# A fused Mamba-2 scan and SiLU MLP on one Trainium2 core: weight clipping on GpSimd, a wider-row load of C, and a later product for one unit

## The chip, the core and the metric

The kernel runs on one core of one Trainium2 chip. The core has five engines that run side by side and meet at semaphores: TensorE (PE in the profile, its weight loads PEld), VectorE (DVE), ScalarE (ACT), GpSimd (POOL) and SyncE (SP), which issues most DMAs here. The metric is the device time of one execution in microseconds (us); lower is better. The kernel before has a median of 353.54 us in three runs (353.08 to 353.58).

## The reference

Two blocks follow each other. The first is a state-space scan over 4 batches, 8 heads and 768 tokens with head dimension D = 32 and state dimension N = 16; the second is a two-matrix MLP with SiLU between.

```python
# x (4, 8, 768, 32), a (4, 8, 768), B and C (4, 8, 768, 16): float32
log_a = log(clip(a, 1e-6, 1)); state = 0
for each chunk of tokens:
    cum   = cumsum(log_a in the chunk)
    L     = exp(cum_i - cum_j) for i >= j, else 0
    y     = ((C B^T) * L) x  +  (C state) * exp(cum_i)      # "decay" of C by the prefix product
    state = exp(sum log_a) * state + sum_j B_j x_j exp(cum_last - cum_j)
# bridge: (batch, head, token, D) -> (batch*token, head*D), 3072 x 256
h = y @ w_in            # w_in  (256, 2048), float64
g = h / (1 + exp(-h))
out = g @ w_out         # w_out (2048, 256), float64; out 3072 x 256 in float32
```

The two weight matrices arrive as float64, so the kernel turns each of them into float32 on the chip, bit by bit.

## The kernel before

The 3072 tokens are cut into 12 units of 256 tokens, three to a batch (`UPB = 3`). Unit 0 opens batch 0, units 1 and 2 continue it, unit 3 opens batch 1. For each unit the scan part makes `XM[u]` (the y of that unit), and two MLP products follow. The first MLP product is `f_s1`; the second comes in steps of one matmul from a generator and is taken with `f_s2(n)`. Weights are handled in 16 pieces, 0 to 7 of `w_in` and 8 to 15 of `w_out`. `f_s1(g, j)` needs `w_in` piece j.

Loads. `load_n` brings B (i = 0) or C (i = 1) with tokens on partitions, so each run in memory is one head's 16 numbers of one token: 64 bytes. `load_t` brings them with 8 tokens to a partition row: 512 bytes to a run.

```python
def load_n(u, i, q):
    b, t0 = at(u)
    if i == 0:
        t = bn[u] = loads.tile([128, 2, H, N], FP32, name="bn")
    else:
        t = tbc[u] = loads.tile([128, 2, 2, 8, N], FP32, name="tbc")[:, 0]
    for k in range(2):
        q.dma_start(out=t[:, k], in_=(B, C)[i][b, :, t0 + 128 * k:t0 + 128 * k + 128].rearrange("h p n -> p h n"))

def load_t(u, i, q):
    b, t0 = at(u)
    if i == 0:
        tbc[u] = loads.tile([128, 2, 2, 8, N], FP32, name="tbc")
    for g in range(4):
        q.dma_start(out=tbc[u][32 * g:32 * g + 32, i],
                    in_=(B, C)[i][b, 2 * g:2 * g + 2, t0:t0 + UT].rearrange("e (t r) n -> t e r n", r=8))

def load_unit(u):
    load_pa(u, nc.sync)
    if 0 < u < UPB:
        load_n(u, 1, nc.sync)
    else:
        load_t(u, 0, nc.sync)
        load_t(u, 1, nc.sync)
    load_ab(u, nc.sync)
    load_n(u, 0, nc.sync)
    load_x(u, nc.sync)
```

Weights. Two ScalarE operations make a magnitude `u` and a low part `v`; VectorE clips u, shifts it and merges the sign into v; GpSimd adds the two as integers.

```python
def w_size(n):
    u = wu[n] = wtp.tile([128, 2, WF], FP32, name="wu")
    v = wv[n] = wtp.tile([128, 2, WF], FP32, name="wv")
    nc.scalar.activation(u, raw[n][:, :, :, 1].bitcast(FP32), AF.Abs)
    nc.scalar.activation(v, raw[n][:, :, :, 0], AF.Copy, scale=2.0 ** -51, bias=2.0)

def w_bits(n, parts=1):
    # ... u, v, hi and dst are the tiles of piece n
    nc.vector.tensor_scalar(out=u, in0=u, scalar1=LEAST, scalar2=MOST, op0=ALU.max, op1=ALU.min)       # clip, L174
    nc.vector.tensor_scalar(out=u, in0=u, scalar1=3, scalar2=None, op0=ALU.logical_shift_left)         # shift, L176
    nc.vector.scalar_tensor_tensor(out=v, in0=hi, scalar=0x80000000, in1=v,
                                   op0=ALU.bitwise_and, op1=ALU.bitwise_or)                            # sign, L178
    for i in range(parts):
        nc.gpsimd.tensor_tensor(out=dst[:, :, fs].bitcast(U32), in0=u[:, :, fs], in1=v[:, :, fs], op=ALU.add)  # L182
    if n + RAW < len(W):
        load_w(n + RAW, nc.sync)
```

The scan's use of B and C. `f_T` is a VectorE transpose, `f_TP` a TensorE transpose into PSUM (units 1 and 2 alone), `f_C` multiplies C by the prefix product of a. `f_P0`, `f_P1` make that prefix product, `f_E0`, `f_E1`, `f_Ek` make the decay matrix E by scans on VectorE, `f_B` decays B on GpSimd, `f_D0` and `f_G0` are small matmuls, `f_S` carries the state, `f_SM` masks it on ScalarE, `f_M` multiplies E into the product, `f_Y` is the matmul for y, and `f_X` copies y out of PSUM.

```python
def f_T(u, i):
    t = (BH, CT)[i][u] = sc.tile([128, UT], FP32, name=("bh", "ct")[i])
    nc.vector.transpose(out=t.rearrange("p (t r) -> p r t", r=8), in_=tbc[u][:, i].rearrange("p e r n -> p r e n"))
    if i == 1:
        tbc.pop(u)

def f_TP(u):
    tp = ps_o.tile([128, 512], FP32, name="o_ps")
    for i, t in enumerate((bn[u], tbc.pop(u))):
        for k in range(2):
            nc.tensor.transpose(out=tp[:, 256 * i + 128 * k:256 * i + 128 * k + 128],
                                in_=t[:, k].rearrange("p h n -> p (h n)"), identity=ident)
    BH[u] = sc.tile([128, UT], FP32, name="bh")
    nc.scalar.activation(BH[u], tp[:, 0:256], AF.Copy)
    CT[u] = tp[:, 256:512]

def f_C(u):
    CW[u] = sc.tile([128, UT], FP32, name="cw")
    engine = nc.vector if 0 < u < UPB else nc.gpsimd
    engine.tensor_tensor(out=CW[u].rearrange("p (c t) -> p c t", t=Q),
                         in0=CT.pop(u).rearrange("p (c t) -> p c t", t=Q), in1=PFX[u][:, :, 1:], op=ALU.mult)
```

The order of issue at the start is written by hand, and each engine keeps it:

```python
# ... unit 0's transposes, G0, E, B, D0, P, C before this
f_S(0); f_SM(0)
for k in range(2): f_M(0, k)
w_size(0); w_bits(0, 2)
f_Ab(1, 0); w_size(1); busy(4, 17)
f_Y(0); f_Ab(1, 1); f_X(0)
w_size(2); w_bits(1); load_unit(2)
f_s1(0, 0)
f_Ek(1, 0); f_TP(1)
for e in range(2): f_T2(1, e)
f_s1(0, 1)
f_Ek(1, 1); f_B(1); w_bits(2); f_C(1); f_D0(1, True); f_G0(1); f_S(1); f_SM(1)
w_size(3)
for k in range(2): f_M(1, k)
f_s1(0, 2); w_size(4); w_bits(3); w_bits(4)
f_Y(1); f_X(1); w_size(5)
f_s1(0, 3)
# then f_s1 of units 0 and 1 in turn, with weight pieces (s = w_size, b = w_bits) and unit 2's scan between:
steps = ((1, 0, "b5 s6"), (1, 1, "b6 s7"), (1, 2, "b7 s8"), (1, 3, "b8"), (0, 4, "E D"),
         (1, 4, ""), (0, 5, "T C s9"), (1, 5, "b9 s10"), (0, 6, "G"), (1, 6, "b10 s11"),
         (0, 7, "Y b11 s12"), (1, 7, "b12 s13"))
```

The stage in which units 4 and 5 are scanned while unit 3 goes through its first product:

```python
for j in range(8):
    # ...
    f_s1(3, j)
    scan_piece(4, j, ("TE", "DCS", "G", "YS", "", "", "", ""))
    scan_piece(5, j, ("", "", "T", "E", "DCS", "G", "YS", ""))
    # ...
    f_s2(2 if j in (5, 6) else 4)
```

Of the kernel before, what the change touches and what calls it, by code (L numbers as in the profile page):

```python
# [8 lines left out]
FP32 = mybir.dt.float32  # L9
U32 = mybir.dt.uint32  # L10
BF16 = mybir.dt.bfloat16
AF = mybir.ActivationFunctionType
ALU = mybir.AluOpType
# [8 lines left out]
def kernel(  # L22
# [26 lines left out]
    Q = 64  # L49
# [46 lines left out]
                        in_=bass.AP(tensor=a.tensor, offset=a.offset + b * H * S + t0 + t * Q,  # L96
                                    ap=[[0, 64], [S, H], [1, Q]]))

    def load_n(u, i, q):

        b, t0 = at(u)
        if i == 0:
            t = bn[u] = loads.tile([128, 2, H, N], FP32, name="bn")
        else:
            t = tbc[u] = loads.tile([128, 2, 2, 8, N], FP32, name="tbc")[:, 0]
        for k in range(2):
            q.dma_start(out=t[:, k], in_=(B, C)[i][b, :, t0 + 128 * k:t0 + 128 * k + 128].rearrange("h p n -> p h n"))  # L107

    def load_t(u, i, q):

        b, t0 = at(u)
        if i == 0:
            tbc[u] = loads.tile([128, 2, 2, 8, N], FP32, name="tbc")
        for g in range(4):
            q.dma_start(out=tbc[u][32 * g:32 * g + 32, i],
                        in_=(B, C)[i][b, 2 * g:2 * g + 2, t0:t0 + UT].rearrange("e (t r) n -> t e r n", r=8))
# [6 lines left out]

    def load_unit(u):
        load_pa(u, nc.sync)
        if 0 < u < UPB:
            load_n(u, 1, nc.sync)
        else:
            load_t(u, 0, nc.sync)
            load_t(u, 1, nc.sync)  # L130
        load_ab(u, nc.sync)
        load_n(u, 0, nc.sync)
        load_x(u, nc.sync)

    w_in_sb = const.tile([128, KC, d_ff], FP32, name="w_in_sb")
# [24 lines left out]
    def w_size(n):  # L160
        if n in raw:
# [3 lines that stand above are left out]

            nc.scalar.activation(v, raw[n][:, :, :, 0], AF.Copy, scale=2.0 ** -51, bias=2.0)

    def w_bits(n, parts=1):
        dst = w_piece(n)[1]
        if n in raw:  # L170
            u, v, hi = wu.pop(n), wv.pop(n).bitcast(U32), raw[n][:, :, :, 1]


            nc.vector.tensor_scalar(out=u, in0=u, scalar1=LEAST, scalar2=MOST, op0=ALU.max, op1=ALU.min)  # L174
            u = u.bitcast(U32)
            nc.vector.tensor_scalar(out=u, in0=u, scalar1=3, scalar2=None, op0=ALU.logical_shift_left)  # L176

            nc.vector.scalar_tensor_tensor(out=v, in0=hi, scalar=0x80000000, in1=v,  # L178
                                           op0=ALU.bitwise_and, op1=ALU.bitwise_or)
            for i in range(parts):  # L180
                fs = slice(WF // parts * i, WF // parts * (i + 1))
# [3 lines that stand above are left out]
# [10 lines left out]
    pz01, one01, pfx01 = (flat[:, 8 * UT + QZ * i:8 * UT + QZ * (i + 1)] for i in range(3))  # L195
    load_t(0, 0, nc.scalar)
    load_t(0, 1, nc.sync)
    load_n(0, 0, nc.scalar)
    nc.sync.dma_start(out=pa01, in_=bass.AP(tensor=a.tensor, offset=a.offset, ap=[[S, H], [0, N], [1, 2 * UT]]))
    load_x(0, nc.sync)  # L200
    for n in range(3):
        load_w(n, nc.sync)
    load_n(1, 0, nc.sync)
    load_n(1, 1, nc.sync)
    load_x(1, nc.sync)

    mark = const.tile([1, RAW], U32, name="mark")
# [107 lines left out]
    def f_Ek(u, k):  # L315
        scan_E(u, H * k, H, ab.pop((u, k)))
# [26 lines left out]
# [7 lines that stand above are left out]
    def f_TP(u):  # L350

        tp = ps_o.tile([128, 512], FP32, name="o_ps")
        for i, t in enumerate((bn[u], tbc.pop(u))):
            for k in range(2):
                nc.tensor.transpose(out=tp[:, 256 * i + 128 * k:256 * i + 128 * k + 128],
                                    in_=t[:, k].rearrange("p h n -> p (h n)"), identity=ident)
        BH[u] = sc.tile([128, UT], FP32, name="bh")
        nc.scalar.activation(BH[u], tp[:, 0:256], AF.Copy)
        CT[u] = tp[:, 256:512]

    def f_T2(u, e):

# [4 lines left out]
    def f_C(u):  # L367

        CW[u] = sc.tile([128, UT], FP32, name="cw")
        engine = nc.vector if 0 < u < UPB else nc.gpsimd  # L370
        engine.tensor_tensor(out=CW[u].rearrange("p (c t) -> p c t", t=Q),
                             in0=CT.pop(u).rearrange("p (c t) -> p c t", t=Q), in1=PFX[u][:, :, 1:], op=ALU.mult)

    def f_D0(u, early=False):

# [41 lines left out]
    def f_S(u, t0=0, t1=4):  # L417

        first, last = u % UPB == 0, u % UPB == UPB - 1
        if first and t0 == 0:  # L420
            ST[u] = sc2.tile([128, 4, 64], FP32, name="st")
        if not last and t1 == 4:
            ST[u + 1] = sc2.tile([128, 4, 64], FP32, name="st")
        for t in range(t0, min(t1, 3 if last else 4)):
            k, c = divmod(t, 2)
            o = ST[u][:, t + 1] if t < 3 else ST[u + 1][:, 0]
            if first and t == 0:
                nc.vector.tensor_copy(out=o, in_=BX[u][c][:, k])
            else:
                nc.vector.scalar_tensor_tensor(out=o, in0=ST[u][:, t], scalar=PFX[u][:, t, Q:],  # L430
                                               in1=BX[u][c][:, k], op0=ALU.mult, op1=ALU.add)

    def f_SM(u):

        t0 = 1 if u % UPB == 0 else 0
        SM[u] = sc.tile([128, 4, 64], FP32, name="sm")
        for e in range(2):
            nc.scalar.activation(SM[u][:, t0:, 32 * e:32 * e + 32], ST[u][:, t0:, 32 * e:32 * e + 32],
                                 AF.Copy, scale=par[:, e:e + 1])
# [43 lines left out]
    def f_s1(g, j):  # L483
        if j == 0:
            GTS[g] = new_g()
        xm = XM[g].rearrange("p (w c) t -> p w (c t)", w=2)
        hp = ps_h.tile([128, 2, UT], FP32, name="hp")
        for i in range(2):
            f = 2 * j + i
            for kc in range(KC):  # L490
                nc.tensor.matmul(out=hp[:, i], lhsT=w_in_sb[:, kc, f * 128:(f + 1) * 128],  # L491
                                 rhs=xm[:, kc], start=(kc == 0), stop=(kc == KC - 1))
        nc.scalar.activation(GTS[g][:, :, j], hp, AF.Silu)  # L493
        if j == 7:
            XM.pop(g)
# [243 lines left out]
    def scan_piece(u, j, plan):  # L739
        for what in plan[j]:  # L740
            if what == "E":
                f_P(u)
                f_E(u)
            elif what == "T":
                if u < UPB:
                    f_TP(u)
                else:
                    f_T(u, 0)
                    f_T(u, 1)
                f_T2(u, 0)  # L750
                f_T2(u, 1)
            elif what == "t":
                f_T(u, 0)
                f_T(u, 1)
            elif what == "B":
                f_B(u)
                f_C(u)
            elif what == "D":
                f_B(u)
            elif what == "C":  # L760
                f_C(u)
            elif what == "S":
                f_SW(len(SW))
            elif what == "G":
                f_GMD(u)
            elif what == "Y":
                f_Y(u)
                f_X(u)
# [34 lines left out]
    f_D0(0, True)  # L803
    f_P01()
    f_C(0)
    f_S(0)
    f_SM(0)
    for k in range(2):
        f_M(0, k)
    w_size(0)  # L810
    w_bits(0, 2)
    f_Ab(1, 0)
    w_size(1)
    busy(4, 17)
    f_Y(0)
    f_Ab(1, 1)
    f_X(0)
    w_size(2)
    w_bits(1)
    load_unit(2)  # L820
    f_s1(0, 0)
    f_Ek(1, 0)
    f_TP(1)
    for e in range(2):
        f_T2(1, e)
    f_s1(0, 1)
    f_Ek(1, 1)
    f_B(1)
    w_bits(2)
    f_C(1)  # L830
    f_D0(1, True)
    f_G0(1)
    f_S(1)
# [62 lines left out]
    for j in range(8):  # L896
        waiting, PEND[:] = PEND[:], []
        f_s1(3, j)
        scan_piece(4, j, ("TE", "DCS", "G", "YS", "", "", "", ""))
        scan_piece(5, j, ("", "", "T", "E", "DCS", "G", "YS", ""))  # L900
        scan_piece(6, j, ("",) * 7 + ("t",))
        if j == 7:
            for i in range(4):
                f_XT(2, i)

        f_s2(2 if j in (5, 6) else 4)
        if j == 3:
            f_SO(3)
        outputs(waiting)
        if j == 5:  # L910
            f_T1(1, 0)
            f_T1(1, 1)
            f_TS(1, 3, 0)
        if j in (2, 5):
            load_unit(6 + j // 3)
# [67 lines left out]
```

## Time and profile before

| what | value |
|---|---|
| time, median of three runs | 353.54 us |
| span of the profiled execution | 353.3 us |
| TensorE busy | 343.8 us (97%) |
| VectorE busy | 204.4 us (58%) |
| ScalarE busy | 162.0 us (46%) |
| GpSimd busy | 111.5 us (32%) |
| mean DMA rate | 121 GB/s |
| TensorE busy from 0 to 30 us of the span | 25.8 us |
| TensorE busy from 60 to 340 us | 279.76 us |

How to read it. A busy share is an average over the whole span. The last two rows, from the stage table, cut it in two: the opening has gaps on TensorE, the long middle hardly any. In the timeline each row gives the start in us, the time from the first start to the last end of the merged instructions, the engine, the line of the kernel, what is written from what, and how many; in square brackets stands how long the engine had been idle and who released it. A row marked SPq is the issue of a DMA on SyncE's queue, not the transfer.

### The profile page before, as it was taken

To read this page: it belongs to the slowest core of one execution; us is meant where nothing else is said; L and a number is where in the kernel's file an instruction comes from. 1 tells how busy PE (TensorE), PEld (TensorE's weight loads), DVE (VectorE), ACT (ScalarE), POOL (GpSimd) and SP (SyncE) were. 2 spreads that over 40 slices of the span, in tenths; PEclk is the share of its full clock that TensorE was granted. 3 is DMA by queue.
4 is the path that set the end of the run, shared out by engine and by line. 5 is a ranking of instruction groups with operands and counts; after the bars stand their busy time and mean duration, and the time that the engine had idled before them with its cause. 6 is when DMAs were issued, how large, how long until landed. Compare 5 with 4: busy or idle time off the path is not lost.

```text
span 353.3 us, 8349 instructions
## 1 busy us (share of the span) xinstructions
PE 343.8 (97%) x3308; PEld 287.5 (81%) x3308; DVE 204.4 (58%) x408; ACT 162.0 (46%) x394; POOL 111.5 (32%) x137
## 2 busy tenths in 40 slices
PE   8979999999999999999999999999999999999995
PEld 3658778888888888888888888888888888888883
DVE  6997879978586663553664563564652232234821
ACT  2567487233323645454645445544545454453100
POOL 4344335554085041244041244041234112051200
PEclk9999999999999999999999999999999999999999
DMA  6986895699649398958179956057404237522202
GB/s 107 225 243 161 174 371 108 125 194 210 132 99 154 81 185 164 184 104 147 32 146 185 172 98 105 16 98 143 92 2 74 51 61 142 90 46 38 36 4 46
DMA packets 117376, 42.79 MB, mean 121 GB/s; under 512 B 102488, under 2 KB 109144, under 8 KB 117336
## 3 DMA queue, kind: packets, MB, share of 16 engines
q1 hardware_dynamic: 110328, 25.67, 34.7%
q0 software_dynamic: 4464, 16.25, 24.9%
q10 hardware_dynamic: 2544, 0.33, 0.6%
q8 instruction: 26, 0.43, 0.6%
q14 instruction: 14, 0.11, 0.1%
HBM read 22.83 MB, written 3.15 MB: 74 GB/s over the span
## 4 chain that ended last, share of the span: by engine, by line
PE 75%; DVE 9%; DMA 8%; SPq 5%; issue 2%; ACT 0%; ACTq 0%; DVEq 0%
PE o_ps L627 32%; PE hp L682 28%; PE hp L491 4%; PE hp L627 3%; DMA out_dram<-ot 2%; DMA ab<-in_a_dram 2%; SPq L95 2%; PE o_ps L613 2%; PE gy L467 2%; DVE E L303 1%; DVE E L415 1%; DMA raw<-in_moe_w_out_dram 1%; SPq L107 1%; PE gy L458 1%; DMA gT<-in_a_dram 1%
## 5 line engine op out<-in xcount | busy, mean ns | idle before, releaser
L685 DVE TENSOR_TENSOR gT<-hp,p 128x256 f32<-128x256 f32 x64 | 26.9, 420 | 73.8 <-ACT p L696 37.9
L491 PE MATMUL hp<-XM,w_in_sb 128*128 128x256 f32 x256 | 59.6, 382 | 2.0 <-POOL w_in_sb L182 2.0
L627 PE MATMUL o_ps<-gT,w_out_sb 128*128 128x256 f32 x240 | 60.4, 379 | 0.0
L688 ACT ACTIVATE gT<-gT 128x256 f32<-128x256 f32 x96 | 39.7, 414 | 44.0 <-DVE gT L685 43.9
L491 PEld LDWEIGHTS hp<-XM,w_in_sb 128*128 128x128 f32 x256 | 47.9, 190 | 10.0 <-POOL w_in_sb L182 3.3
L682 PE MATMUL hp<-raw 128*128 128x256 f32 x192 | 52.7, 380 | 0.0
L544 POOL TENSOR_TENSOR ps<-ps 128x256 f32<-128x256 f32 x35 | 29.2, 835 | 72.3 <-ACT ps L574 71.0
L627 PEld LDWEIGHTS o_ps<-gT,w_out_sb 128*128 128x128 f32 x240 | 45.4, 190 | 6.3
L539 POOL DMA_DIRECT2D gT<-gT x31 | 27.4, 921 | 64.9 <-PE hp L682 22.3
L682 PEld LDWEIGHTS hp<-raw 128*128 128x128 f32 x192 | 36.2, 190 | 5.4 <-POOL ps L544 0.6
L696 ACT ACTIVATE p<-hp 128x256 f32<-128x256 f32 x64 | 24.5, 383 | 27.5 <-PE hp L682 26.1
L685 DVE TENSOR_TENSOR gT<-hp,u 128x256 f32<-128x256 f32 x32 | 13.6, 425 | 39.3 <-PE hp L682 39.3
L682 PE MATMUL hp<-XM,w_in_sb 128*128 128x256 f32 x128 | 34.1, 389 | 0.0
L493 ACT ACTIVATE gT<-hp 128x512 f32<-128x512 f32 x32 | 19.0, 594 | 28.3 <-PE hp L491 28.2
L682 PEld LDWEIGHTS hp<-XM,w_in_sb 128*128 128x128 f32 x128 | 23.3, 190 | 4.3 <-issue 1.0
L303 DVE TENSOR_TENSOR_SCAN E<-ab,diag 128x256 f32<-128x256 f32 (+1 forms) x32 | 25.6, 842 | 0.4
L574 ACT ACTIVATE ps<-o_ps 128x256 f32<-128x256 f32 x38 | 14.4, 382 | 23.9 <-PE o_ps L627 22.2
L340 POOL TENSOR_TENSOR BT<-bn,E 128x256 f32<-128x256 f32 x12 | 9.0, 748 | 50.2 <-DVE E L303 48.9
L627 PE MATMUL o_ps<-gT,wu 128*128 128x256 f32 x88 | 22.4, 380 | 0.0
L627 PE MATMUL o_ps<-gT,wv 128*128 128x256 f32 x88 | 22.2, 380 | 0.0
L627 PE MATMUL o_ps<-gT,raw 128*128 128x256 f32 x80 | 20.6, 382 | 0.0
L682 PE MATMUL hp<-raw,w_in_sb 128*128 128x256 f32 x64 | 19.1, 380 | 0.0
(125 smaller groups left out, 518.7 us busy)
## 6 DMA issues: line engine op xcount, KB each, us to landing
gT<-gT POOLq DMA_DIRECT2D x31, 512.0 KB, 6.0
ab<-in_a_dram SPq DMA_DIRECT2D x40, 128.0 KB, 3.9
raw<-in_moe_w_in_dram SPq DMA_DIRECT2D x8, 512.0 KB, 6.3
raw<-in_moe_w_out_dram SPq DMA_DIRECT2D x8, 512.0 KB, 6.5
xt<-in_x_dram SPq DMA_DIRECT2D x24, 128.0 KB, 5.7
out_dram<-ot SPq DMA_DIRECT2D x92, 32.0 KB, 2.5
bn<-in_B_dram SPq DMA_DIRECT2D x22, 64.0 KB, 4.8
tbc<-in_C_dram SPq DMA_DIRECT2D x40, 32.0 KB, 1.8
```

What stands on the lines that cost most here:

```text
L303: nc.vector.tensor_tensor_scan(out=E[u].rearrange("p k h t -> p (k h t)")[:, Q * g0:Q * (g0 + n)], data0=t.rearrange("p g t -> p (g t)"), ...
L340: engine.tensor_tensor(out=BT[u], in0=bn[u], in1=E[u][:, :, :, Q - 1:Q].to_broadcast([128, 2, H, N]), op=ALU.mult)
L491: nc.tensor.matmul(out=hp[:, i], lhsT=w_in_sb[:, kc, f * 128:(f + 1) * 128], rhs=xm[:, kc], start=(kc == 0), stop=(kc == KC - 1))
L493: nc.scalar.activation(GTS[g][:, :, j], hp, AF.Silu)
L539: nc.gpsimd.dma_start(out=o[:, js], in_=a[:, js], accum_op=ALU.add)
L544: engine.tensor_tensor(out=o, in0=p, in1=q, op=op)
L574: nc.scalar.activation(pn, on, AF.Copy)
L627: nc.tensor.matmul(out=o, lhsT=w(j), rhs=g()[:, j], start=(j == 0), stop=(j == last))
L682: nc.tensor.matmul(out=o, lhsT=w, rhs=x_, start=start, stop=True, skip_group_check=True)
L685: nc.vector.tensor_tensor(out=o, in0=p, in1=q, op=ALU.add)
L688: nc.scalar.activation(o, i, AF.Silu)
L696: nc.scalar.activation(o, i, AF.Copy)
```

## The change

It has four parts. First, GpSimd clips the weight pieces 0, 1 and 2 in place of VectorE, and the ScalarE operations of pieces 0 and 1 move ahead in the order of issue. Second, C of units 1 and 2 (unit 3 had it already) is loaded in runs of 512 bytes by `load_t` in place of 64 bytes by `load_n`. Third, that C is then transposed by VectorE into SBUF in place of by TensorE into PSUM, and GpSimd in place of VectorE multiplies it by the prefix product. Fourth, in the stage of units 4 and 5, two matmuls of the second product are issued ahead of the scan's parts in each step, so that the scan's matmuls, unit 5's y among them, come later in TensorE's order. It is meant to take work from VectorE at the start, to shorten the loads of units 1 and 2, and to let unit 5's y find its inputs ready.

The diff, with blank lines taken out:

```diff
--- before.py
+++ after.py
@@ -96,20 +96,17 @@
                         in_=bass.AP(tensor=a.tensor, offset=a.offset + b * H * S + t0 + t * Q,
                                     ap=[[0, 64], [S, H], [1, Q]]))
-    def load_n(u, i, q):
+    def load_n(u, q):
         b, t0 = at(u)
-        if i == 0:
-            t = bn[u] = loads.tile([128, 2, H, N], FP32, name="bn")
-        else:
-            t = tbc[u] = loads.tile([128, 2, 2, 8, N], FP32, name="tbc")[:, 0]
+        bn[u] = loads.tile([128, 2, H, N], FP32, name="bn")
         for k in range(2):
-            q.dma_start(out=t[:, k], in_=(B, C)[i][b, :, t0 + 128 * k:t0 + 128 * k + 128].rearrange("h p n -> p h n"))
+            q.dma_start(out=bn[u][:, k], in_=B[b, :, t0 + 128 * k:t0 + 128 * k + 128].rearrange("h p n -> p h n"))
     def load_t(u, i, q):
         b, t0 = at(u)
-        if i == 0:
+        if u not in tbc:
             tbc[u] = loads.tile([128, 2, 2, 8, N], FP32, name="tbc")
         for g in range(4):
             q.dma_start(out=tbc[u][32 * g:32 * g + 32, i],
@@ -123,13 +120,11 @@
     def load_unit(u):
         load_pa(u, nc.sync)
-        if 0 < u < UPB:
-            load_n(u, 1, nc.sync)
-        else:
+        if u >= UPB:
             load_t(u, 0, nc.sync)
-            load_t(u, 1, nc.sync)
+        load_t(u, 1, nc.sync)
         load_ab(u, nc.sync)
-        load_n(u, 0, nc.sync)
+        load_n(u, nc.sync)
         load_x(u, nc.sync)
     w_in_sb = const.tile([128, KC, d_ff], FP32, name="w_in_sb")
@@ -165,14 +160,18 @@
             nc.scalar.activation(v, raw[n][:, :, :, 0], AF.Copy, scale=2.0 ** -51, bias=2.0)
-    def w_bits(n, parts=1):
+    def w_clip(n, engine):
+
+
+        if n in raw:
+            engine.tensor_scalar(out=wu[n], in0=wu[n], scalar1=LEAST, scalar2=MOST, op0=ALU.max, op1=ALU.min)
+
+    def w_bits(n, parts=1, clip=True):
         dst = w_piece(n)[1]
         if n in raw:
-            u, v, hi = wu.pop(n), wv.pop(n).bitcast(U32), raw[n][:, :, :, 1]
-
-
-            nc.vector.tensor_scalar(out=u, in0=u, scalar1=LEAST, scalar2=MOST, op0=ALU.max, op1=ALU.min)
-            u = u.bitcast(U32)
+            if clip:
+                w_clip(n, nc.vector)
+            u, v, hi = wu.pop(n).bitcast(U32), wv.pop(n).bitcast(U32), raw[n][:, :, :, 1]
             nc.vector.tensor_scalar(out=u, in0=u, scalar1=3, scalar2=None, op0=ALU.logical_shift_left)
             nc.vector.scalar_tensor_tensor(out=v, in0=hi, scalar=0x80000000, in1=v,
@@ -195,13 +194,13 @@
     pz01, one01, pfx01 = (flat[:, 8 * UT + QZ * i:8 * UT + QZ * (i + 1)] for i in range(3))
     load_t(0, 0, nc.scalar)
     load_t(0, 1, nc.sync)
-    load_n(0, 0, nc.scalar)
+    load_n(0, nc.scalar)
     nc.sync.dma_start(out=pa01, in_=bass.AP(tensor=a.tensor, offset=a.offset, ap=[[S, H], [0, N], [1, 2 * UT]]))
     load_x(0, nc.sync)
     for n in range(3):
         load_w(n, nc.sync)
-    load_n(1, 0, nc.sync)
-    load_n(1, 1, nc.sync)
+    load_n(1, nc.sync)
+    load_t(1, 1, nc.sync)
     load_x(1, nc.sync)
     mark = const.tile([1, RAW], U32, name="mark")
@@ -350,13 +349,11 @@
     def f_TP(u):
         tp = ps_o.tile([128, 512], FP32, name="o_ps")
-        for i, t in enumerate((bn[u], tbc.pop(u))):
-            for k in range(2):
-                nc.tensor.transpose(out=tp[:, 256 * i + 128 * k:256 * i + 128 * k + 128],
-                                    in_=t[:, k].rearrange("p h n -> p (h n)"), identity=ident)
+        for k in range(2):
+            nc.tensor.transpose(out=tp[:, 128 * k:128 * k + 128], in_=bn[u][:, k].rearrange("p h n -> p (h n)"),
+                                identity=ident)
         BH[u] = sc.tile([128, UT], FP32, name="bh")
         nc.scalar.activation(BH[u], tp[:, 0:256], AF.Copy)
-        CT[u] = tp[:, 256:512]
     def f_T2(u, e):
@@ -367,9 +364,8 @@
     def f_C(u):
         CW[u] = sc.tile([128, UT], FP32, name="cw")
-        engine = nc.vector if 0 < u < UPB else nc.gpsimd
-        engine.tensor_tensor(out=CW[u].rearrange("p (c t) -> p c t", t=Q),
-                             in0=CT.pop(u).rearrange("p (c t) -> p c t", t=Q), in1=PFX[u][:, :, 1:], op=ALU.mult)
+        nc.gpsimd.tensor_tensor(out=CW[u].rearrange("p (c t) -> p c t", t=Q),
+                                in0=CT.pop(u).rearrange("p (c t) -> p c t", t=Q), in1=PFX[u][:, :, 1:], op=ALU.mult)
     def f_D0(u, early=False):
@@ -746,7 +742,7 @@
                     f_TP(u)
                 else:
                     f_T(u, 0)
-                    f_T(u, 1)
+                f_T(u, 1)
                 f_T2(u, 0)
                 f_T2(u, 1)
             elif what == "t":
@@ -803,31 +799,35 @@
     f_D0(0, True)
     f_P01()
     f_C(0)
+    w_size(0)
+    w_clip(0, nc.gpsimd)
     f_S(0)
     f_SM(0)
+    w_size(1)
+    w_clip(1, nc.gpsimd)
     for k in range(2):
         f_M(0, k)
-    w_size(0)
-    w_bits(0, 2)
+    w_bits(0, 2, False)
     f_Ab(1, 0)
-    w_size(1)
     busy(4, 17)
     f_Y(0)
     f_Ab(1, 1)
     f_X(0)
     w_size(2)
-    w_bits(1)
+    w_bits(1, 1, False)
     load_unit(2)
     f_s1(0, 0)
+    f_T(1, 1)
     f_Ek(1, 0)
     f_TP(1)
     for e in range(2):
         f_T2(1, e)
+    f_C(1)
+    w_clip(2, nc.gpsimd)
     f_s1(0, 1)
     f_Ek(1, 1)
     f_B(1)
-    w_bits(2)
-    f_C(1)
+    w_bits(2, 1, False)
     f_D0(1, True)
     f_G0(1)
     f_S(1)
@@ -896,14 +896,15 @@
     for j in range(8):
         waiting, PEND[:] = PEND[:], []
         f_s1(3, j)
+
+        f_s2(2)
         scan_piece(4, j, ("TE", "DCS", "G", "YS", "", "", "", ""))
         scan_piece(5, j, ("", "", "T", "E", "DCS", "G", "YS", ""))
         scan_piece(6, j, ("",) * 7 + ("t",))
         if j == 7:
             for i in range(4):
                 f_XT(2, i)
-
-        f_s2(2 if j in (5, 6) else 4)
+        f_s2(0 if j in (5, 6) else 2)
         if j == 3:
             f_SO(3)
         outputs(waiting)
```

## The prediction

> **What bounds the kernel now.** I read the page's busy shares first, then the stage table, then TensorE's timeline at each gap, then the waits and the SyncE queue behind them.
>
> ```profile
> PE 343.8 (97%) x3308; PEld 287.5 (81%) x3308; DVE 204.4 (58%) x408; ACT 162.0 (46%) x394; POOL 111.5 (32%) x137
> ...
> 15.00:20.00 5.00, 4.66 (x22) 3.29 (x20) 4.97 (x7) 2.89 (x7) 3.13 (x4) 1.00 0.94 161
> 20.00:25.00 5.00, 4.07 (x142) 3.12 (x144) 4.60 (x12) 3.32 (x7) 1.37 (x2) 1.00 0.71 233
> 25.00:30.00 5.00, 4.27 (x62) 3.67 (x49) 4.54 (x6) 3.09 (x7) 2.54 (x2) 1.00 0.90 271
> 30.00:35.00 5.00, 5.00 (x25) 4.41 (x24) 3.02 (x7) 4.55 (x9) 2.56 (x2) 1.00 0.50 103
> ```
>
> The columns after the stage and its length are PE, PEld, DVE, ACT and POOL. TensorE is the bound: 97% over all and 279.76 of 280 us from 60 to 340. Only gaps can be won, and work that leaves TensorE inside the full stretch. From 15 to 30 us VectorE is at 4.5 to 5.0 of 5 and TensorE is not: VectorE paces the start. TensorE's timeline names the gaps:
>
> ```profile
> 18.14 1.99 PE L491 MATMUL hp<-XM,w_in_sb 128*128 128x256 f32 x8 [0.34 <-POOL w_in_sb L182]
> ...
> 22.07 1.99 PE L491 MATMUL hp<-XM,w_in_sb 128*128 128x256 f32 x8 [0.94 <-POOL w_in_sb L182]
> ...
> 26.21 1.99 PE L491 MATMUL hp<-XM,w_in_sb 128*128 128x256 f32 x8 [0.73 <-POOL w_in_sb L182]
> ...
> 40.59 0.75 PE L355 MATMUL o_ps<-ident,bn 128*128 128x128 f32 x2 [0.30 <-DMA bn<-in_B_dram]
> 41.18 0.38 PE L355 MATMUL o_ps<-ident,tbc 128*128 128x128 f32 x2
> 41.39 3.62 PE L491 MATMUL hp<-XM,w_in_sb 128*128 128x256 f32 x16
> ...
> 50.15 0.69 PE L458 MATMUL gy<-cw,sm 32*64 32x64 f32 x32 [0.50 <-DVE E L415]
> ...
> 107.96 0.69 PE L458 MATMUL gy<-cw,sm 32*64 32x64 f32 x32 [0.24 <-DVE E L415]
> ```
>
> Three waits for weight pieces 1, 2 and 3 make 0.34 + 0.94 + 0.73 = 2.01 us; unit 2 has 0.30 (B not landed) and 0.50 (its E late); unit 5 has 0.24. Together 3.05 us: with the transposes taken out, nearly all that this change can bring. Behind unit 2's gaps stands SyncE's queue:
>
> ```profile
> 10.53 4.62 SPq L107 DMA_DIRECT2D tbc<-in_C_dram  x2
> ...
> 25.50 4.97 SPq L107 DMA_DIRECT2D tbc<-in_C_dram  x2
> 30.52 5.94 SPq L95 DMA_DIRECT2D ab<-in_a_dram  x4
> 36.50 1.25 SPq L107 DMA_DIRECT2D bn<-in_B_dram  x2
> 37.79 2.82 SPq L122 DMA_DIRECT2D xt<-in_x_dram  x2
> 40.71 4.13 SPq L156 DMA_DIRECT2D raw<-in_moe_w_out_dram  x7
> ```
>
> The two issues of C take 4.62 and 4.97 us, and what follows waits in line: unit 2's a and B, and pieces 9 to 15. The chain of waits runs through just these rows.
>
> [...] the two-input add of 128x512 takes 1303 ns, a one-input select of that size 670. The clip itself has not run there yet[...]. [...] the shift (L176) takes 0.43 us alone and 1.39 us beside an add. [...] four 512-byte C issues of later units take 1.83 us, two 64-byte ones 4.6 to 5.0. [...] Here GpSimd's rows show SBUF operands only.
>
> **The change, part by part.**
>
> Clips. Between the end of unit 0's E product (12.98) and the start of unit 1's (22.13) VectorE loses three clips of 0.42 and the decay of C of 0.41, and gains a transpose of 0.64: 1.26 + 0.41 - 0.64 = 1.03 us less. GpSimd gains 3 x 0.75 + 0.68 = 2.9 us; its rows between 11.4 and 22.0 hold 1.72 + 1.27 + 0.68 + 1.26 = 4.9 of 10.6 us, so there is room. But the order costs. Unit 0's x is there at 10.07 (its matmul's wait ends); the weights follow it, and 512 KB at the 380 GB/s that the DMA view shows then is 1.4 us, so piece 0 lands at about 11.45. ScalarE, which did the mask first at 11.50, now does the two operations of piece 0 (12.05 to 13.27 before, so 1.22 us) and then the mask: done at 13.3 in place of 12.14. Unit 0's y started at 13.10, so it loses about 0.25. Piece 1's magnitude follows at 14.0, GpSimd clips it to about 14.8, and only then adds piece 0's first half, to 15.65 (0.86 each; before 15.32). The first product then starts near 15.7, not 15.39: 0.3 later. VectorE's shift of piece 1 waits for the same clip and then falls beside the adds[...]. GpSimd also has C and clip 2 (1.4 us) ahead of unit 1's B, which frees D0 and the state. So of the 1.03 us perhaps a third comes through to the product at 26.21. I take **0.3 us**, between a loss of 0.3 and a gain of 0.9.
>
> C in wide rows. Each C load of units 1 and 2 goes from two issues (4.62, 4.97) to four of about 0.43, 1.7 us: 2.9 and 3.2 us less on the queue, some 6 us in all for what follows unit 2's C, less what the backlog of weight transfers takes back. B of unit 2 is ready before 40: **0.30**. Its a lands before 40.45, where VectorE waited 0.78, and piece 9, for which ScalarE waited 3.02 to 45.79, comes some 5 us earlier; piece 9's bits no longer hold back the state and E of unit 2, and the gap before its y goes: **0.50**.
>
> Transposes. From the start at 40.59 to the next product at 41.39 four transposes took 0.80 us, in the full stretch. Two remain, about 0.35: **0.45**. Unit 1's pair (17.42 to 17.80) lies in the gap before 18.14: nothing. VectorE's extra 0.64 - 0.40 for unit 2 lies beside products.
>
> Unit 5's y. Both the small matmuls that start its state and its y move back by two matmuls (0.87 us). The state step began at 105.71, late because VectorE was at work on another sum until 105.78, not because of TensorE (done at 104.93); so E stays ready at about 107.8 while y comes at 108.6: **0.24** gained.
>
> Sum: 0.3 + 0.30 + 0.50 + 0.45 + 0.24 = 1.79 us. 353.54 - 1.79 = 351.75; I say 351.7. From 60 us on nothing else moves but by being earlier; the last 13 us stay as they are.
>
> **Rivals.** (1) *GpSimd becomes the pace-setter of the start*: the clips sit in its order ahead of adds and of unit 1's B, and ScalarE's new order delays the mask. For it: the waits just worked out, and VectorE, busy 4.5 to 5.0 of every 5 us there[...]. Against it: GpSimd's room. It would take the 0.3 and up to 0.5 more: about 352.5. (2) *VectorE's saving comes through whole*: piece 0 lands by 10.8, clips take 0.67. Then products 1 to 3 gain about 1 us: 351.0, and down to 350.4 if earlier weights help too. (3) *The earlier loads are hidden anyway, or collide*: the queue's stall on C may be the backlog of 2 MB of weights issued from 22.0 to 24.7, and the next issue then stalls in its place. Then unit 2's 0.8 shrinks to about 0.3: 352.3. Against it: 4.62 us on C of unit 1 while fewer weights waited. (4) *TensorE, being earlier, meets work that is not ready* from 50 to 80 us, where VectorE is at 98% in the first ten. Against it: the last weight piece is added at 64.5 and used after 67; the sum for the fifth product ends at 68.1 and is used at 70.66.
>
> **Range and chances.** The parts that don't depend on order (unit 2's transposes, unit 5) give 0.7; all gaps closed give 3.5. A loss at the start of 0.5 with unit 2's gain missed leaves 353.0; everything right gives 350.4. Two per cent would be 7 us, twice all gaps, so both outer chances are near nothing.
>
> **What would show it.** TensorE's waits for weight pieces, 2.01 us before, should stay between 1 and 2.3; the product of 26.21 should start between 25.3 and 26.5. The C issues should be four of 0.4 each; no wait for B at 40; the gap before unit 2's y gone; no 0.24 before unit 5's y; TensorE's transposes reading B alone. GpSimd's clip should take 0.65 to 0.85 us. The prediction is wrong if that clip is two-input slow (1.3 us), if the first product starts after 16.3, if the wide C load takes as long to issue as the narrow one, or if a new wait opens between 50 and 80 us.

## The result: slower by 1.7%, and the profile after

The changed kernel takes 358.74 us (358.35 to 360.07, five runs) where the kernel before takes 353.08 (352.87 to 353.58): a ratio of 1.0167, 95% interval 1.0143 to 1.0192. The prediction was 351.7, between 350.4 and 353.0. It missed in size and in sign.

The page of the changed kernel, its TensorE row and the row of the clock granted to TensorE:

```profile
PE 346.6 (97%) x3303; PEld 289.1 (81%) x3304; DVE 203.8 (57%) x405; ACT 162.4 (45%) x394; POOL 117.0 (33%) x142
...
PEclk9989999999989999999999999999999999999999
```

The busy share is the same 97%. But there are fewer matmuls and more busy time than before, and the clock row has two slices of 8 (the 3rd is the opening, the 12th lies near 100 us). TensorE's timeline has the gaps that answer to those shown before:

```profile
16.25 2.00 PE L487 MATMUL hp<-XM,w_in_sb 128*128 128x256 f32 x8 [1.03 <-POOL w_in_sb L181]
18.09 0.38 PE L353 MATMUL o_ps<-ident,bn 128*128 128x128 f32 x2
19.33 1.97 PE L487 MATMUL hp<-XM,w_in_sb 128*128 128x256 f32 x8 [0.85 <-DVE E L302]
22.16 0.46 PE L385 MATMUL hp<-xt,BT 64*32 64x64 f32 x32 [0.87 <-POOL BT L339]
...
24.39 3.51 PE L487 MATMUL hp<-XM,w_in_sb 128*128 128x256 f32 x8 [1.14 <-POOL w_in_sb L181]
27.82 0.69 PE L454 MATMUL gy<-cw,sm 32*64 32x64 f32 x32
...
29.23 14.08 PE L487 MATMUL hp<-XM,w_in_sb 128*128 128x256 f32 x64
43.15 0.38 PE L353 MATMUL o_ps<-ident,bn 128*128 128x128 f32 x2
43.37 3.62 PE L487 MATMUL hp<-XM,w_in_sb 128*128 128x256 f32 x16
...
99.11 2.06 PE L623 MATMUL o_ps<-gT,w_out_sb 128*128 128x256 f32 x4 [2.14 <-ACT ps L570]
101.11 1.13 PE L454 MATMUL gy<-cw,sm 32*64 32x64 f32 x32
...
113.98 0.69 PE L454 MATMUL gy<-cw,sm 32*64 32x64 f32 x32
```

Piece 3's product starts at 29.23, not 26.21. The product of piece 2 takes 3.51 us where each other one takes 1.97 to 2.00: half of the lateness is speed, not waiting. Unit 2 has no gap (43.15, 43.37) and unit 5's y has none (113.98), as forecast. But there is a wait of 2.14 us at 99.11 that the kernel before did not have, and again the two matmuls after it (four instructions) are slow: 2.06 us, where two others of this kernel take 1.13 (at 94.12).

The same timeline for GpSimd and VectorE in the opening (L167 is the clip, L175 the shift, L181 the add, L339 unit 1's B):

```profile
11.70 3.81 POOL L167 TENSOR_SCALAR wu<-wu 128x512 f32<-128x512 f32 x2 [0.67 <-ACT wu L159]
...
13.65 0.83 DVE L175 TENSOR_SCALAR wu<-wu 128x512 uint32<-128x512 uint32 x1 [1.00 <-POOL wu L167]
...
15.48 1.59 POOL L181 TENSOR_TENSOR w_in_sb<-wu,wv 128x256 uint32<-128x256 uint32 x2
15.54 0.95 DVE L175 TENSOR_SCALAR wu<-wu 128x512 uint32<-128x512 uint32 x1 [0.45 <-POOL wu L167]
...
19.58 1.92 POOL L167 TENSOR_SCALAR wu<-wu 128x512 f32<-128x512 f32 x1
21.46 0.65 POOL L339 TENSOR_TENSOR BT<-bn,E 128x256 f32<-128x256 f32 x1
21.54 0.86 DVE L175 TENSOR_SCALAR wu<-wu 128x512 uint32<-128x512 uint32 x1 [1.24 <-POOL wu L167]
```

One clip takes 1.92 us on GpSimd, against 0.42 on VectorE. Two of them stand back to back ahead of piece 0's adds, and the shift of piece 0 starts only when the first is over (13.65); the third stands ahead of unit 1's B, which its matmuls wait for until 22.16 (20.06 before). VectorE, which was to be relieved, stands idle 1.00, 0.45 and 1.24 us for the clips.

At 97 us it is ScalarE's order that explains the wait. Its timeline in the changed kernel:

```profile
95.30 0.69 ACT L434 ACTIVATE sm<-st,par 128x128 f32<-128x128 f32 x2 [2.35 <-DVE st L426]
97.89 0.91 ACT L362 ACTIVATE ce<-ct,par 128x256 f32<-128x256 f32 x2 [1.89 <-DVE ct L345]
98.70 0.36 ACT L570 ACTIVATE ps<-o_ps 128x256 f32<-128x256 f32 x1
```

The copy that empties `o_ps` (L570) stands behind the two operations on unit 5's transposed C (L362), which wait for VectorE until 97.89. There is only one `o_ps` buffer, and two matmuls of the next segment now come ahead of unit 4's y and need it 1.4 us earlier than before. In the kernel before the same copy stood behind the same two operations, and came just in time for the matmul at 96.78:

```profile
95.50 0.91 ACT L365 ACTIVATE ce<-ct,par 128x256 f32<-128x256 f32 x2 [1.90 <-PE hp L491]
96.31 0.36 ACT L574 ACTIVATE ps<-o_ps 128x256 f32<-128x256 f32 x1
96.78 1.99 PE L627 MATMUL o_ps<-gT,w_out_sb 128*128 128x256 f32 x8
```

Counted from the start of the product ahead of it (93.55 before, 95.08 after), the copy is 0.86 us later (2.76 before, 3.62 after), because unit 4's small matmuls, and with them VectorE's state step and transposes, also stand behind two matmuls more. 1.4 and 0.9, less the 0.1 there was to spare, make 2.2, where 2.14 was measured.

The stage table of this execution for both places (after the stage and its length: PE, PEld, DVE, ACT, POOL, then the granted clock):

```profile
22.00:25.00 3.00, 1.70 (x66) 1.28 (x67) 2.83 (x8) 1.02 (x3) 1.37 (x2) 0.85 0.60 193
25.00:28.00 3.00, 3.00 (x18) 2.18 (x20) 1.76 (x4) 0.87 (x3) 1.13 (x1) 0.59 0.83 251
...
96.00:100.00 4.00, 1.86 (x7) 1.32 (x6) 3.97 (x8) 1.66 (x4) 0.86 (x1) 0.90 0.82 141
100.00:104.00 4.00, 4.00 (x103) 2.97 (x103) 1.69 (x3) 0.60 (x1) 2.80 (x4) 0.68 0.41 101
```

Right after each stretch in which TensorE was about half idle (busy 1.70 of 3 us and 1.86 of 4), the clock is 0.59 and 0.68 for some microseconds. No single gap between matmuls in these stretches is longer than the 2.14 us at 99.11. What brings the lower clock on is not shown by this trace; the fillers below test whether the idle time does.

### The profile page after: what moved, and what is told of

It is laid out like the page before. It is cut to its first block, busy times and chain, and to the rows that moved or that the text cites. A ratio compares the mean times of both kernels' runs of the same rounds, so it can differ in the third digit from the quotient of the medians.

```text
span 358.2 us, 8352 instructions
## 1 busy us (share of the span) xinstructions
PE 346.6 (97%) x3303; PEld 289.1 (81%) x3304; DVE 203.8 (57%) x405; ACT 162.4 (45%) x394; POOL 117.0 (33%) x142
## 4 chain that ended last, share of the span: by engine, by line
PE 88%; DMA 2%; POOL 2%; DVE 2%; issue 2%; ACT 1%; SPq 1%; ACTq 0%; DVEq 0%; POOLq 0%
PE o_ps L623 35%; PE hp L678 28%; PE hp L487 14%; PE hp L623 3%; PE gy L463 2%; PE gy L454 2%; PE o_ps L609 2%; PE gy L400 2%; POOL wu L167 2%; DMA raw<-in_moe_w_in_dram 1%; PE gy L385 1%; DMA tbc<-in_B_dram 1%; DVE wv L177 1%; POOL w_in_sb L181 1%; ACT ce L362 1%
## 5 line engine op out<-in xcount | busy, mean ns | idle before, releaser
L487 PE MATMUL hp<-XM,w_in_sb 128*128 128x256 f32 x256 | 61.3, 390 | 3.0 <-POOL w_in_sb L181 2.2
L623 PE MATMUL o_ps<-gT,w_out_sb 128*128 128x256 f32 x240 | 61.6, 384 | 2.1 <-ACT ps L570 2.1
L487 PEld LDWEIGHTS hp<-XM,w_in_sb 128*128 128x128 f32 x256 | 48.8, 194 | 11.7 <-POOL w_in_sb L181 4.3
L540 POOL TENSOR_TENSOR ps<-ps 128x256 f32<-128x256 f32 x35 | 28.0, 801 | 73.1 <-ACT ps L570 68.9
L678 PE MATMUL hp<-XM,w_in_sb 128*128 128x256 f32 x128 | 34.1, 389 | 0.0
L678 PEld LDWEIGHTS hp<-XM,w_in_sb 128*128 128x128 f32 x128 | 23.3, 190 | 4.3 <-issue 1.0
L570 ACT ACTIVATE ps<-o_ps 128x256 f32<-128x256 f32 x38 | 14.5, 383 | 23.9 <-PE o_ps L623 19.8
L339 POOL TENSOR_TENSOR BT<-bn,E 128x256 f32<-128x256 f32 x12 | 9.1, 758 | 48.3 <-DVE E L302 32.4
```

The source lines that it names most:

```text
L339: engine.tensor_tensor(out=BT[u], in0=bn[u], in1=E[u][:, :, :, Q - 1:Q].to_broadcast([128, 2, H, N]), op=ALU.mult)
L540: engine.tensor_tensor(out=o, in0=p, in1=q, op=op)
L570: nc.scalar.activation(pn, on, AF.Copy)
L623: nc.tensor.matmul(out=o, lhsT=w(j), rhs=g()[:, j], start=(j == 0), stop=(j == last))
L678: nc.tensor.matmul(out=o, lhsT=w, rhs=x_, start=start, stop=True, skip_group_check=True)
```

## The experiments

A ratio compares all runs of a kernel with the runs of the kernel before made at the same time, not two medians; the medians before are 353.05 for the first four experiments, 352.97 for the next four and 353.37 for the last four.

My theory after the result: two separate losses, GpSimd's slow clips and the copy of `o_ps`, each made dearer by the clock, and a small gain from C. The first four runs take the change apart.

**C and the steps, with the clips on VectorE.**

```diff
-    w_size(0); w_clip(0, nc.gpsimd); f_S(0); f_SM(0); w_size(1); w_clip(1, nc.gpsimd)   # and w_clip(2, nc.gpsimd)
-    for k in range(2): f_M(0, k)
-    w_bits(0, 2, False)
+    f_S(0); f_SM(0)
+    for k in range(2): f_M(0, k)
+    w_size(0); w_bits(0, 2)                                                             # w_size(1) after f_Ab(1, 0)
```

> The changed kernel with the clips of pieces 0, 1 and 2 back on VectorE and the old order of ScalarE; C and the step order stay changed. Theory (the loss is two separate ones: slow clips at the start, worth about 3 us of which half is TensorE's lower clock, and a new wait on the only o_ps buffer near 97 us, worth about 3.5 us with its clock): about 355.5 us, product of piece 3 starting near 26.3, the o_ps wait of 2.1 us still there. Rival (the wide C load collides with the weight loads and that delays the start): still 358 to 359. Rival (the o_ps wait is only a consequence of the late start): 353 or less.

356.86 us; ratio 1.0103 (1.0059 to 1.0148). Piece 3's product starts at 26.86; the waits of TensorE still hold this line:

```profile
PE o_ps L623 <- ACT ps L570: 2.1, 1, 2.1
```

So the wait doesn't come from the late start. The time is 1.4 above my figure. In the execution profiled the clock stayed at 1.00 after this wait, and it took 355.82; the other three have a mean clock of 0.993 to 0.997 and took 356.76 to 357.22.

**C and the clips, with the old steps.**

```diff
-        f_s2(2)                          # ahead of the scan pieces
-        f_s2(0 if j in (5, 6) else 2)
+        f_s2(2 if j in (5, 6) else 4)    # behind them
```

> The changed kernel with the old order of second-product steps in the stage of units 4 and 5; the clips stay on GpSimd. Theory (two separate losses): about 355.2 us, no wait on o_ps near 97 us and no low clock after it, the 0.24 us wait before unit 5's y back, the start as late as in the changed kernel. Rival (the whole loss comes from the late start): still 358 to 359.

356.47 us; ratio 1.0087 (1.0055 to 1.0120). The start is as late as in the changed kernel (29.17), the `o_ps` wait is gone. The time is 1.3 above my figure, and the 0.24 before unit 5's y, which I expected back, is not in this trace.

**C alone** (both edits above).

> Only the C part of the change: wide rows, transposed by VectorE, decayed by GpSimd; clips and step order as before the change. Theory (two separate losses, and C gains about 1.5 us at unit 2, less 0.2 for one more VectorE transpose at the start): 351.6 to 352.2 us, faster than the kernel before. Rival (the loads collide): above 354.

353.38 us; ratio 1.0006 (0.9992 to 1.0020): no gain that can be told, and 1.2 above the top of what the theory said. The loads don't collide, but neither does anything come of them. SyncE's, VectorE's and TensorE's rows of this kernel say where it went:

```profile
10.28 5.46 SPq L112 DMA_DIRECT2D tbc<-in_C_dram  x4
...
17.26 0.65 DVE L345 STREAM_TRANSPOSE ct<-tbc 128x256 f32<-128x256 f32 x1 [0.88 <-DMA tbc<-in_C_dram]
...
19.06 1.97 PE L487 MATMUL hp<-XM,w_in_sb 128*128 128x256 f32 x8 [1.83 <-DVE E L302]
```

The four wide issues of unit 1's C take 5.46 us, longer than the two narrow ones (4.62): what holds the queue there is not C's own short rows. C lands late, VectorE's transpose stands in its order ahead of unit 1's E and waits 0.88 us for it, and piece 1's product comes at 19.06 in place of 18.14.

**The clips alone**, on the kernel before.

> Only the clips of pieces 0, 1 and 2 on GpSimd, with the new order of ScalarE; all else as before the change. Theory: 355.5 to 356.5 us, GpSimd's clip 1.9 us each, the product of piece 3 near 29. Rival (clips are only slow together with the decay of C on GpSimd): about 354.

354.26 us; ratio 1.0035 (1.0025 to 1.0046), nearer to the rival's figure than to mine. But the rival's reason fails: clips take 1.92 us here too, and piece 3's product starts at 27.89. So the clips are slow without C's help, but they cost 3.1 us on top of C (356.47 - 353.38) and 1.2 without it. With C, the decay of C (0.69) and the third clip both stand ahead of unit 1's B; the gaps are longer (0.86 us for unit 1's B, against 0.49), and the clock gives way in all five runs of the kernel with C, the clips and the old steps (mean 0.992 to 0.995). Of the 20 runs of the clips alone, seven have a mean clock of 0.993 or 0.994 and a median of 354.97; the other thirteen have 353.96. So a fall of the clock goes with about 1.0 us more; it doesn't explain every long run, as two of the thirteen took 354.73 and 354.95 at a mean clock of 1.00.

The next four test the mechanisms.

**The copy first.** On C with the new steps and VectorE's clips:

```diff
         scan_piece(4, j, ("TE", "DCS", "G", "YS", "", "", "", ""))
+        if j == 2:
+            f_s2(2)
         scan_piece(5, j, ("", "", "T", "E", "DCS", "G", "YS", ""))
-        f_s2(0 if j in (5, 6) else 2)
+        f_s2(0 if j in (2, 5, 6) else 2)
```

> C part and new step order, clips on VectorE, and in step 2 of the stage of units 4 and 5 the second pair of second-product matmuls goes ahead of unit 5's transposes, so that ScalarE's copy out of the only o_ps buffer stands ahead of its two operations on those transposes. Theory (the 2.1 us wait is this copy standing in ScalarE's order behind work that waits for VectorE): the wait is gone, and the time falls from 356.9 to about 353.2, the level of C alone. Rival (the wait comes from the order of TensorE alone, as the next segment is asked for earlier than any copy could be done): 356 to 357.

353.40 us; ratio 1.0013 (1.0003 to 1.0023). The wait is gone, and 3.5 us with it (356.86 - 353.40). In the trace TensorE's order at this place is the one it was, and the two matmuls that waited start at 94.13, 1.73 us after the start of the product ahead of them (92.40; 4.03 in the changed kernel, from 95.08 to 99.11). What the edit moves is the copy, ahead of unit 5's two operations. So the wait was ScalarE's order, and with it gone no other cost of the new steps can be told (C alone has 353.38).

**One operation in the clip**, on the clips alone:

```diff
-            engine.tensor_scalar(out=wu[n], in0=wu[n], scalar1=LEAST, scalar2=MOST, op0=ALU.max, op1=ALU.min)
+            engine.tensor_scalar(out=wu[n], in0=wu[n], scalar1=LEAST, scalar2=None, op0=ALU.max)   # on GpSimd
```

> Clips of pieces 0 to 2 alone on GpSimd, and there only the lower bound is taken; the upper bound is left out for these pieces, which would matter only for weights above 2^16 times 1.875. Theory (GpSimd pays for each of the two operations of a clip): one takes about 1.0 us in place of 1.92 and the time falls from 354.3 to about 353.2. Rival (the cost is that of moving 128x512 through GpSimd, whatever is done): 1.9 us again and 354.3.

353.21 us; ratio 1.0003 (0.9994 to 1.0012). The line of the clip itself (least, median and greatest duration in ns), first in the changed kernel, which clips the other pieces on VectorE, then here:

```profile
L167 DVE TENSOR_SCALAR wu<-wu x13: 412/416/1496, 25.3 to 62.2; 128x512 f32<-128x512 f32 x13
L167 POOL TENSOR_SCALAR wu<-wu x3: 1905/1922/1924, 11.7 to 19.6; 128x512 f32<-128x512 f32 x3
```

```profile
L171 POOL TENSOR_SCALAR wu<-wu x3: 1484/1495/1641, 11.9 to 18.6; 128x512 f32<-128x512 f32 x3
```

The time is what the theory said, the duration isn't: the second operation is worth 0.43 us, not half, and 1.5 us stay. Taking 3 x 0.43 = 1.3 us off GpSimd takes 1.05 us off the kernel (0.75 against the thirteen runs above at 353.96). Piece 3's product starts at 27.12 in place of 27.89, 0.77 earlier, so GpSimd's clips are the path of that start.

**Fillers.** On C with the clips and the old steps:

```diff
+    busy(3)
     f_D0(1, True)
     f_G0(1)
+    busy(5)
```

> Clips on GpSimd with C changed and the old step order, and eight filler matmuls, whose result nobody reads, in TensorE's gaps before unit 1's D0 and before the product of piece 2. Theory (TensorE's lower clock after 24 us is brought on by the idle time before it): clock 0.998 to 1.0 in place of 0.993, the product of piece 2 takes 2.0 us in place of 3.1, time about 355.0 in place of 356.5. Rival (the clock falls for another reason, or at random): no change or slower by the fillers, 356.5 to 357.

355.41 us; ratio 1.0065 (1.0049 to 1.0080), against 356.47 without them. The stage tables, first without and then with fillers:

```profile
22.00:25.00 3.00, 1.80 (x67) 1.42 (x68) 2.83 (x8) 1.13 (x3) 1.26 (x1) 1.00 0.68 218
25.00:28.00 3.00, 3.00 (x30) 2.02 (x33) 1.65 (x4) 1.27 (x4) 1.24 (x1) 0.50 0.85 266
```

```profile
22.00:25.00 3.00, 3.00 (x73) 1.85 (x74) 2.83 (x8) 1.24 (x4) 1.26 (x1) 1.00 0.73 235
25.00:28.00 3.00, 2.59 (x103) 1.95 (x101) 2.13 (x5) 2.39 (x6) 1.28 (x1) 1.00 0.89 289
```

Eight useless matmuls make the kernel 1.06 us faster: the clock stays at 1.00, and piece 2's product takes 1.99 us in place of 3.11. All four runs are below all five without fillers. 2.0 us are left above C alone (355.41 - 353.38); the traces show 1.04 of them as the later start of piece 3's product (27.99 against 26.95), and where the rest lies is not shown.

**The kernel before, once more.**

> The kernel before, unchanged, for a second profile. The first profile was of an execution of 355.06 us, above the median of 353.1. If unit 2's gaps of 0.30 and 0.50 us belong to that execution alone, this profile lacks them and its piece-3 product starts near 26; that would say why C alone gained nothing. If they are always there, C's gain was lost elsewhere.

353.48 us. TensorE's timeline at the places on which the prediction rested:

```profile
26.00 14.08 PE L491 MATMUL hp<-XM,w_in_sb 128*128 128x256 f32 x64 [0.73 <-POOL w_in_sb L182]
39.99 0.56 PE L355 MATMUL o_ps<-ident,bn 128*128 128x128 f32 x2
40.39 0.38 PE L355 MATMUL o_ps<-ident,tbc 128*128 128x128 f32 x2
...
48.90 0.69 PE L458 MATMUL gy<-cw,sm 32*64 32x64 f32 x32
...
106.70 0.69 PE L458 MATMUL gy<-cw,sm 32*64 32x64 f32 x32 [0.23 <-DVE E L415]
```

The 0.30 at unit 2's B and the 0.50 before its y are not there. The first profile's execution took 355.06 us against a median of 353.05; the clips alone, the one-operation clip and the later unit 5 below keep the old loads of unit 2, and their traces lack both gaps too. Unit 5's 0.23 is there. But it isn't always: of the traces with the old steps, the two of the kernel before and the one-operation clip have it, and the other five (the clips alone and C alone among them) don't.

The last four look for a better kernel.

**Only unit 5 later**, on the kernel before:

```diff
+        if j in (5, 6):
+            f_s2(2)
         scan_piece(4, j, ...)
-        f_s2(2 if j in (5, 6) else 4)
+        f_s2(0 if j in (5, 6) else 4)
```

> The kernel before, with only unit 5's small matmuls and y behind two matmuls of the second product in steps 5 and 6; units 4's steps stay as before, so no segment of the second product is asked for earlier. Theory (the 0.23 us wait before unit 5's y is in every execution and this alone removes it): 352.7 to 352.8 where before has 353.0. Rival (something else takes up the 0.23): 353.0.

353.17 us where before had 353.37; ratio 0.9997 (0.9987 to 1.0007). The trace has no such wait, but five traces with the old steps have none either, and the time can't tell.

**Also C of unit 2 alone**: `f_TP`, `f_C` and the loads take the new way for u = 2, the old for u = 1.

> The former, and C of unit 2 alone in wide rows, transposed by VectorE and decayed by GpSimd; unit 1's C stays with TensorE and narrow rows. Theory (C's gain is the pair of transposes that leaves TensorE at unit 2, 0.22 us, and its loss lies at unit 1): 352.4 to 352.6. Rival (VectorE's transpose at unit 2 costs what it brings): as the former or slower.

353.11 us; ratio 1.0003 (0.9989 to 1.0016): no gain that can be told. Its profiled execution, of 354.44 us, had a wait of 0.87 for unit 2's B and one of 0.31 before its y, with C in wide rows: the wide load doesn't keep these gaps away.

**C alone, with unit 1's C ahead of piece 2:**

```diff
-    for n in range(3):
+    for n in range(2):
         load_w(n, nc.sync)
-    load_n(1, nc.sync)
     load_t(1, 1, nc.sync)
+    load_w(2, nc.sync)
+    load_n(1, nc.sync)
```

> C alone, with unit 1's wide C load issued ahead of weight piece 2. Theory (C alone lost at the start because VectorE waited 0.88 us for C of unit 1, stuck behind the weights, ahead of unit 1's E): no such wait, the product of piece 3 starts 0.5 to 0.9 us earlier than in C alone, time 352.6 to 352.9 in place of 353.4. Rival (the extra transpose on VectorE is the cost, not the wait): 353.2 to 353.4.

352.97 us; ratio 0.9989 (0.9981 to 0.9998). SyncE's and VectorE's rows:

```profile
8.40 1.88 SPq L112 DMA_DIRECT2D tbc<-in_C_dram  x4
...
16.72 0.63 DVE L346 STREAM_TRANSPOSE ct<-tbc 128x256 f32<-128x256 f32 x1
```

The same four issues take 1.88 us with less queued ahead of them, the transpose waits for nothing, piece 1's product still waits 0.55 us for E (1.83 in C alone), and piece 3's product starts at 26.39 in place of 26.95. The intervals of the two ratios still overlap a little, so that the earlier load makes the kernel faster than C alone is likely, not shown.

**Both together.**

> The former with unit 5's y later in steps 5 and 6 only. Theory (the gains add): 352.4 to 352.7, 0.2 below the former. Rival (no gain from unit 5): as the former.

352.66 us; ratio 0.9985 (0.9978 to 0.9992). It beats the kernel before by 0.15% and the changed kernel by 6 us. Whether unit 5's part adds to it is not settled: the intervals of this kernel and the previous one overlap.

## Why the prediction was wrong

- **Clips: the step that failed most.** The term was "3 x 0.75 + 0.68 = 2.9 us" on GpSimd. The 0.75 was only an estimate of mine: the trace had no clip on GpSimd, and the nearest to it was a select of the same size, at 0.67. Measured: 1.92 a clip, so 5.8 + 0.69 us in the same 10.6; even with one operation the clip takes 1.50. The path that I worked out was right (clips ahead of adds and of B, shifts waiting for clips), and with 1.92 in it the gain of 0.3 turns into a loss: rival 1, but much stronger than my "up to 0.5 more". Its part is about 2 us besides the clock (fillers against C alone), of which 1.0 is seen at the start. The prediction named a clip of 1.3 us as what would make it wrong.
- **The clock was not in the sum at all.** All gaps were counted at their length. About 1.0 us of the clips' loss is TensorE at half speed afterwards, shown by the fillers (from 25 to 28 us the clock is 0.50 without them and 1.00 with them, and they take 1.06 us off the time). But waiting seems the larger part of the whole loss: one of the changed kernel's five runs shows a mean clock of 1.00 and still took 358.35.
- **Unit 5's y.** "0.24 gained" was right of the trace read, not of every trace, and I followed only unit 5 and TensorE. The same edit moves two matmuls of every step ahead of the scan, in step 3 too, and there they meet the single `o_ps` buffer, whose copy waits in ScalarE's order. That is 2.14 us of wait, and 3.5 us of time on C alone (2.4 in the one run whose clock stayed up). My fourth rival named earlier work meeting what is not ready, but between 50 and 80 us and on VectorE.
- **Unit 2's gaps (0.30 + 0.50).** They were not in the second profile. I read them from one execution of 355.06 us, 1.5 above the median of 353.54, with both numbers before me. The path was not shown either: they came back once with the wide load in place.
- **C's issues "four of about 0.43".** They took 4.56 us for unit 1 and 2.66 for unit 2 in the changed kernel: rival 3, and for unit 1 the third of the prediction's signs of being wrong (as long as the narrow load's 4.62). What stands ahead in the queue set the time, as the 1.88 us of the early load shows.
- **Transposes (0.45).** In the second profile four take 0.61 us from start to the next product (39.99 to 40.60); two take 0.22 in the changed kernel. So 0.39 was there to gain, nearly as predicted; in C alone the late landing of unit 1's C, with piece 3's product at 26.95 in place of 26.00, outweighs it.
- **The range.** Its top was mis-summed: a loss of 0.5 at the start, with only the 0.7 that doesn't depend on order, leaves 353.54 + 0.5 - 0.7 = 353.3, not 353.0. Neither end had a term for the clock or for `o_ps`.

The parts don't add: C alone costs 0.3 us (its interval includes none), the clips 3.1 on top, the new steps 2.3 on top of both (358.74 - 356.47) but 3.5 on C alone (356.86 - 353.38). Since the clock falls in some executions and not in others, I can't split the last microsecond.

## What to carry to other kernels

An operation that leaves a full engine for an idle one has to be timed on the new engine in its very form (here 1.92 us a clip, where a select of that size took 0.67), and placed in that engine's order: what stands behind it waits too (here unit 1's B, for which TensorE waited 0.87 us). When matmuls move forward, ask which buffer they need earlier, who empties it, and what that engine has ahead of the copy. Before gaps of a few tenths are added up, take a second profile and look whether its execution is a typical one.

## What the runs showed of the hardware

- GpSimd's two-operation clip of 128x512 float32 took 1.92 us, with one operation 1.50; the two-input integer add of that size took 1.26 to 1.40, a select 0.67, and VectorE's clip 0.42 in the median.
- TensorE's clock fell to about half for some 3 us (0.59 and 0.50 from 25 to 28 us) after seven (18 to 25 us) in which it was busy 4.1 us, with no gap above 1.15 us, in two traces (the changed kernel, and the one with the old steps). With fillers it was busy 5.9 of the seven and the clock stayed at 1.00; so it did in the profiled execution of C alone, at 4.9. It is not certain: among 20 runs of the clips alone, seven have a lower mean clock, and the clock didn't fall after the same 2.1 us wait in one profiled execution (C and the steps: 1.00 from 96 to 104 us).
- Four issues of unit 1's C in 512-byte rows took 5.46 us, and 1.88 us when they were moved ahead of weight piece 2 and of unit 1's B.
